# Unread matmuls that hold the TensorE clock: one per tile, spread evenly, in place of a larger demand with a larger carry

## The chip, the cores and the metric

One NeuronCore of one Trainium2 chip. The time is device microseconds from the first to the last instruction. All runs below are fast (run to run spread up to about 1%). A ratio is the one for runs of both kernels from the same rounds on the same chip; it is not quite the ratio of the medians that stand beside it.

Words used throughout: *cold* is a granted TensorE clock of 0.50 in the trace's clock records, *warm* is 1.00; each change in them lies on a multiple of 3.41 us from the first. A *window* is one such stretch of 3.41 us. A *tile* is one pass of the main loop, mostly three PSUM banks of scores and one exponential over 128x1536. An *unread matmul* is a 128x128 by 512 matmul whose result nobody reads; it is there only to keep the clock up. A *tail* is the chain that normalises a head group (three small TensorE steps with VectorE between, some two tiles apart).

## The reference, cut to what matters

```python
x = A_x                                            # 2048 x 640, bf16; 32 heads of 20
x = x + _A_ref(_layernorm(x), A_wqkv, A_wo)        # layer 0: window of 256 keys
x = x + _B_ref(_layernorm(x), B_wqkv, B_wo)        # layer 1: all 2048 keys, no mask
x = x + _A_ref(_layernorm(x), A_wqkv, A_wo)        # layer 2
x = x + _B_ref(_layernorm(x), B_wqkv, B_wo)        # layer 3
```

## The kernel before

All four layers are woven into one list of tiles. A tile's scores are matmuls of 32 rows (a head of 20, padded), its products with the values matmuls of 21 columns (32\*128 and 128\*21 on the page). A *full-array* matmul, below, is a projection, an output product or an unread matmul: 128\*128 on the page, with 320 or 512 moving columns. Everything else, projections, layernorms and tails, is a list of generators that `pump` advances a little in every tile. The bookkeeping counts full-array work as `heat`, and `keep_clock` adds unread matmuls where it falls short:

```python
def advance(task):
    ...
    state["heat"] += n / 0.22 * (0.15 if task in tails else 0.7 if task.name[0] == "ln" else 1.0)

def keep_clock(least):
    while state["heat"] < least:
        t = choose(False)                       # real work first
        if t is not None and state["credit"] > -0.5:
            state["credit"] -= advance(t)
            continue
        b = min(mfree, key=mfree.get)           # a spare PSUM bank: two early on, then one
        if mfree[b][0] > state["tick"]:
            return                              # taken, by a tail for instance: no unread matmul
        nc.tensor.matmul(ps[:, b, :], lhsT=ident[:], rhs=masks[:, 0, :], start=True, stop=True)
        state["heat"] += 1.0

# in the loop over tiles, after the scores and the exponential of a tile of n_b banks:
    r = rate(t)
    pump(r, r + 0.1)
    ...
    state["heat"] += 0.414 * n_b                # scores and values are counted too
    if woven <= state["unit"] < index[3, 1, 0, None]:   # from layer 1's first tiles to the last layer
        keep_clock(1.0 * n_b - surplus)
    surplus = min(max(surplus + state["heat"] - 1.0 * n_b, 0.0), 1.0 * n_b)
    state["heat"] = 0.0
```

So a tile of three banks asks for 3 - 3 x 0.414 = 1.76 full-array matmuls, and a surplus of up to 3 is carried over.

The softmax here doesn't subtract the row's maximum and nothing guards it: scores larger than these inputs give would overflow.

## Time and profile before

| | before |
|---|---|
| time, median of 3 | 2382.0 us (2379.2 to 2386.25) |
| ScalarE busy | 2183.4 us, 92% of the profiled span of 2378.9 us |
| TensorE busy | 1980.5 us, 83% |
| mean granted clock | 0.82 |
| unread matmuls in the program | 549 |

ScalarE's exponentials are the bound. What is to be won or lost is ScalarE's idle time. The prediction shows the page's lines and the busy times by stage.

### The profile page before, as it was taken

How to read it: one execution, taken by the hardware profiler on the slowest of the kernel's cores; microseconds unless marked ns; L12 is line 12 of the kernel's file. 1: busy time of each engine (PE TensorE's matmuls, PEld its weight loads, DVE VectorE, ACT ScalarE, POOL GpSimd, SP SyncE). 2: the span in 40 equal slices, each digit the busy share in tenths (PEclk: the TensorE clock that was granted, in tenths of full speed). 3: DMA queues.
4: the chain of work that ended last, by engine and by line, in shares of the span. 5: the costliest groups of instructions: out<-in, count | busy, mean ns of one | idle time of the engine just before them, and what ended most of it. 6: DMA issues, size and time to landing. Idle time of an engine off the chain costs nothing. (4 is left out here: it accounts for less than half of the span.)

```text
span 2378.9 us, 39796 instructions
## 1 busy us (share of the span) xinstructions
PE 1980.5 (83%) x15407; PEld 707.1 (30%) x15554; DVE 1458.8 (61%) x2724; ACT 2183.4 (92%) x1739; POOL 142.5 (6%) x295
## 2 busy tenths in 40 slices
PE   7888988878888888778888888887788788888887
PEld 3443333323322332223322333232221121112122
DVE  7576776425646666656666554452567777777774
ACT  7787889898999999999899999999999989999997
POOL 3110110000000001000110001001000000000000
PEclk9898999997988999999997999899755565556557
DMA  6232422322200223102330034112200010001100
GB/s 183 72 101 63 113 67 59 76 70 64 82 19 26 57 67 93 37 14 54 82 98 20 15 82 113 31 33 75 64 29 26 26 37 26 26 27 37 38 14 12
DMA packets 173678, 132.53 MB, mean 56 GB/s; under 512 B 115760, under 2 KB 156080, under 8 KB 173488
## 3 DMA queue, kind: packets, MB, share of 16 engines
q1 hardware_dynamic: 163872, 101.39, 16.9%
q0 software_dynamic: 9616, 28.59, 3.5%
q8 instruction: 122, 2.00, 0.3%
q14 instruction: 68, 0.56, 0.1%
HBM read 98.70 MB, written 27.79 MB: 53 GB/s over the span
## 5 line engine op out<-in xcount | busy, mean ns | idle before, releaser
L1252 ACT ACTIVATE pt<-ps 128x1536 bf16<-128x1536 f32 (+3 forms) x1584 | 2033.7, 1425 | 149.2 <-PE ps L1221 136.9
L1221 PE MATMUL ps<-qt,kt 32*128 32x512 bf16 x4008 | 657.8, 470 | 214.1 <-ACT pt L1252 153.6
L1288 PE MATMUL ps<-pt,vt 128*21 128x512 bf16 x3688 | 473.1, 464 | 22.9 <-DVE oT L810 13.9
L1221 PEld LDWEIGHTS <-kt 32*128 32x128 bf16 x4008 | 188.9, 94 | 622.2 <-issue 601.3
L1318 DVE TENSOR_TENSOR pt<-pt,masks 128x1024 bf16<-128x1024 bf16 (+5 forms) x403 | 238.9, 625 | 133.4 <-ACT pt L1252 132.8
L353 PE MATMUL ps<-xnT,wqk 128*128 128x512 bf16 x760 | 215.6, 395 | 31.1 <-DMA wqk<-in_B_wqkv_dram 8.7
L1288 PEld LDWEIGHTS <-vt 128*21 128x21 bf16 x3960 | 104.0, 90 | 372.3 <-issue 364.1
L304 DVE CAST st<-ps 128x512 bf16<-128x512 f32 x127 | 87.7, 690 | 165.2 <-PE ps L353 164.2
L530 PE MATMUL ps<-wop,on 128*128 128x320 bf16 x976 | 173.1, 322 | 8.0 <-DVE rz L995 2.8
L613 PE MATMUL ps<-masks,ident 128*128 128x512 bf16 x473 | 167.7, 417 | 6.8 <-issue 3.3
L1221 PE MATMUL ps<-qa,ka 32*128 32x384 bf16 (+2 forms) x1408 | 119.1, 280 | 38.0 <-ACT pt L1252 32.7
L1252 ACT ACTIVATE ka<-ps 128x2048 bf16<-128x2048 f32 x68 | 133.6, 1965 | 2.6 <-PE ps L1221 2.2
L858 DVE TENSOR_SCALAR xnT<-ps 128x512 int32<-128x512 f32 x88 | 60.8, 691 | 120.9 <-PE ps L851 119.6
L1020 DVE TENSOR_TENSOR on<-oT,ps 128x512 bf16<-128x512 bf16 x128 | 87.3, 682 | 64.0 <-PE ps L1016 60.8
L539 DVE TENSOR_TENSOR x_sb<-x_sb,ps 128x320 bf16<-128x320 bf16 x120 | 57.8, 482 | 110.0 <-PE ps L530 109.6
L444 PE MATMUL ps<-wv,xnT 128*128 128x320 bf16 x640 | 113.1, 311 | 7.5 <-DVE va L304 1.5
L810 DVE CAST oT<-ps 128x512 bf16<-128x512 f32 x112 | 76.8, 686 | 67.5 <-PE ps L1288 48.1
L530 PEld LDWEIGHTS <-on 128*128 128x128 bf16 x976 | 91.8, 103 | 77.0 <-issue 40.9
L353 PEld LDWEIGHTS <-wqk 128*128 128x128 bf16 x830 | 72.6, 99 | 124.4 <-issue 54.0
L1288 PE MATMUL ps<-pt,va 128*21 128x384 bf16 (+2 forms) x1408 | 78.9, 287 | 10.7 <-DVE oT L810 4.9
L1221 PEld LDWEIGHTS <-ka 32*128 32x128 bf16 x1408 | 44.8, 92 | 106.5 <-issue 97.8
L1288 PE MATMUL ps<-ka,vt 128*21 128x512 bf16 x272 | 70.0, 600 | 2.6 <-DVE oT L810 1.9
(105 smaller groups left out, 1623.7 us busy)
## 6 DMA issues: line engine op xcount, KB each, us to landing
vt<-v_d SPq DMA_DIRECT2D x48, 336.0 KB
kt<-k_d SPq DMA_DIRECT2D x192, 80.0 KB
wqk<-in_B_wqkv_dram SPq DMA_DIRECT2D x80, 160.0 KB
wqk<-in_A_wqkv_dram SPq DMA_DIRECT2D x70, 160.0 KB
k_d<-st POOLq DMA_DIRECT2D x75, 128.0 KB, 2.2
q_d<-st POOLq DMA_DIRECT2D x75, 128.0 KB, 2.1
qt<-q_d SPq DMA_DIRECT2D x384, 20.0 KB
v_d<-vs POOLq DMA_DIRECT2D x16, 336.0 KB, 3.5
```

What stands on the lines that cost most here:

```text
L304: nc.vector.tensor_copy(out=out_, in_=in_)
L353: nc.tensor.matmul(pq, lhsT=wt[:, dc, :], rhs=xt[:, dc, :], start=(dc == 0), stop=(dc == KD - 1),)
L444: nc.tensor.matmul(pv, lhsT=xt[:, dc, i * P : (i + 1) * P], rhs=wv_sb[l % 2][:, dc, h * HD : (h + 1) * HD], start=(dc == 0), stop=(dc == K ...
L530: nc.tensor.matmul(yp, lhsT=on[:, g, qb * P : (qb + 1) * P], rhs=wop[:, g, i * HD : (i + 1) * HD], start=(g == g0), stop=(g == G - 1),)
L613: nc.tensor.matmul(ps[:, b, :], lhsT=ident[:], rhs=masks[:, 0, :], start=True, stop=True)
L810: nc.vector.tensor_copy(out=oT[:], in_=op)
L858: V.tensor_scalar(out=xi.bitcast(I32)[:, i * C : (i + 1) * C], in0=side["psum"], scalar1=SCALE * LOG2E * E23, scalar2=127.0 * E23, op0=ALU ...
L1020: nc.vector.tensor_tensor(out=on[:, g, :], in0=oT[:], in1=zb, op=ALU.mult)
L1221: nc.tensor.matmul(sp[:, i, col * P : (col + qn) * P], lhsT=u.k(kc, j), rhs=u.q(j, q0, qn), start=True, stop=True,)
L1252: nc.scalar.activation(out=pt[:, i:k, b0 * P :], in_=sp[:, i:k, b0 * P :], func=ACT.Exp, scale=SCALE,)
L1288: nc.tensor.matmul(op[32 * j : 32 * j + VW, q0 * P : (q0 + qn) * P], lhsT=u.v(kc, j), rhs=pg[:, i, col * P : (col + qn) * P], start=(first ...
L1318: nc.vector.tensor_tensor(out=pt_[:, i:k, b0 * P :], in0=pt_[:, i:k, b0 * P :], in1=mv_, op=ALU.mult,)
```

## The change

The intent: no tile without a full-array matmul. Scores and values no longer count; every tile of three banks asks for one, in the first layers as well; at most one is carried over; and where a tail holds the spare bank, the unread matmul is written into the tail's own bank just ahead of the tail's result.

```diff
+    def cool():
+        return state["heat"] + state["carry"] < state["least"]
   ... (unread(b): the matmul of before, and heat + 1)
+    def warm_bank(b):
+        if cool() and (
+            state["credit"] <= 0.0 or all(task.wake > state["tick"] for task in todo)
+        ):
+            unread(b)
-    def keep_clock(least):
-        while state["heat"] < least:
+    def keep_clock():
+        while cool():
   ...
+        spare = state["heat"] + state["carry"] - state["least"]
+        state["carry"] = min(max(spare, 0.0), 1.0)
+        state["heat"] = 0.0
   ... (t_tail, at each of its three steps)
         mb = yield from take_m()
+        warm_bank(mb)
   ... (the loop)
+                state["least"] = n_b / 3 if state["unit"] < index[3, 1, 0, None] else 0.0
                 load_ahead()
   ...
-                state["heat"] += 0.414 * n_b
-                if woven <= state["unit"] < index[3, 1, 0, None]:
-                    keep_clock(1.0 * n_b - surplus)
-                surplus = min(max(surplus + state["heat"] - 1.0 * n_b, 0.0), 1.0 * n_b)
-                state["heat"] = 0.0
+                keep_clock()
```

More of the change, by code (lines that the diff above doesn't have):

```diff
@@ L176 @@
     tails = []
-    state = {"tick": 0, "held": None, "credit": 0.0, "early": True, "act": True, "unit": 0, "heat": 0.0}
+    state = {"tick": 0, "held": None, "credit": 0.0, "early": True, "act": True, "unit": 0, "heat": 0.0, "carry": 0.0, "least": 0.0}
     class Task:
@@ L601, in push_layer, with unread @@
                 push(("v", l, c), t_v(l, c, (0, 1)), need[0], 5.6)
-    def keep_clock(least):
-        while state["heat"] < least:
+    def cool():
+        return state["heat"] + state["carry"] < state["least"]
+    def unread(b):
+        nc.tensor.matmul(
+            ps[:, b, :], lhsT=ident[:], rhs=masks[:, 0, :], start=True, stop=True
+        )
+        state["heat"] += 1.0
+    def warm_bank(b):
[5 more added lines that the diff above has]
+        while cool():
             t = choose(False)
@@ L611, in keep_clock @@
             if mfree[b][0] > state["tick"]:
-                return
-            nc.tensor.matmul(
-                ps[:, b, :], lhsT=ident[:], rhs=masks[:, 0, :], start=True, stop=True
-            )
-            state["heat"] += 1.0
+                break
+            unread(b)
+        spare = state["heat"] + state["carry"] - state["least"]
+        state["carry"] = min(max(spare, 0.0), 1.0)
+        state["heat"] = 0.0
     def key_blocks(l, part):
@@ L1004, in t_tail @@
         mb = yield from take_m()
+        warm_bank(mb)
         rp = ps[0:32, mb, :].bitcast(BF16)[:, 0:P]
@@ L1013, in t_tail @@
         mb = yield from take_m()
+        warm_bank(mb)
         zb = ps[:, mb, :]
@@ L1179 @@
         wide_pt = 0
-        surplus = 0.0
         started = set()
```

## The prediction

> **What bounds the kernel now.** I read the page first, its busy times and its 40 slices:
>
> ```profile
> PE 1980.5 (83%) x15407; PEld 707.1 (30%) x15554; DVE 1458.8 (61%) x2724; ACT 2183.4 (92%) x1739; POOL 142.5 (6%) x295
> ...
> ACT  7787889898999999999899999999999989999997
> ...
> PEclk9898999997988999999997999899755565556557
> ```
>
> ScalarE is busy 92% of the span: the exponentials bound the kernel, and time can be won only where ScalarE is idle, 196 us in all (2378.9 less 2183.4). The third line is the clock that the throttle granted to TensorE. It is near full for 28 slices and about half in the last 12, where the kernel asks for no unread matmuls. Next I read busy times by stage (columns: stretch, length, busy us of PE, PEld, DVE, ACT, POOL, clock, DMA share, GB/s):
>
> ```profile
> 0.00:240.00 240.00, 205.22 (x1773) 91.66 (x1793) 162.18 (x402) 179.60 (x223) 46.66 (x110) 0.91 0.38 105
> 240.00:480.00 240.00, 214.04 (x1880) 86.32 (x1907) 147.75 (x311) 212.45 (x184) 28.03 (x54) 0.99 0.30 79
> 480.00:720.00 240.00, 202.07 (x1528) 71.07 (x1549) 119.74 (x243) 227.50 (x186) 10.79 (x20) 0.87 0.22 58
> 720.00:960.00 240.00, 198.36 (x1639) 76.47 (x1657) 153.12 (x290) 226.42 (x179) 16.04 (x32) 0.95 0.24 62
> 960.00:1200.00 240.00, 197.67 (x1644) 75.83 (x1660) 146.48 (x275) 225.36 (x170) 10.64 (x22) 0.94 0.19 48
> 1200.00:1440.00 240.00, 203.63 (x1700) 75.77 (x1720) 141.47 (x277) 225.98 (x170) 14.53 (x29) 0.90 0.23 56
> 1440.00:1690.00 250.00, 202.95 (x1722) 76.38 (x1742) 102.40 (x214) 238.16 (x176) 15.85 (x29) 0.92 0.22 60
> 1690.00:2379.00 689.00, 556.55 (x3545) 153.66 (x3543) 485.62 (x717) 647.91 (x458) 0.00 (x0) 0.56 0.09 29
> ```
>
> ScalarE's idle time is the length less its busy time: 60.4 us in the first stage, 94.1 us from 240 to 1690 us, 41.1 us in the last. The last stage has ScalarE at 94% with the clock at 0.56, so a low clock costs nearly nothing where TensorE has only scores and values to multiply. The change does not touch that stage.
>
> The trace has the clock's records: it is 1.00 or 0.50 and switches at multiples of 3.41 us. Before 240 us there are 5 cold intervals (41 us, ScalarE idle 20.4 us of them). Starting in 240 to 1690 us there are 30 (212 us, ScalarE idle 34.1 us); the warm 1238 us of that stage have 60.0 us idle, 4.8%. At that rate 212 us would have 10.3 us idle anyway, so **cold costs at most about 24 us there**. That is the pot, an estimate from idle time.
>
> What sets the clock? I counted, in each 3.41 us window of the trace, the matmuls that use all 128 rows and columns (512 moving columns = 1). After a warm window with none, the clock fell 26 times in 29; with one, 9 in 26; with two, 7 in 55; with 2.5 to 3, once in 45; with four or more, never. After a cold window the clock rose 5 times in 19 with one, 5 in 19 with two, 5 in 10 with three, 27 in 31 with four or more. Of the seven windows with two that fell, four had only 4 to 6 value matmuls besides, where 8 are usual, so the packed matmuls seem to count a little. One example shows how a hole arises (all engines, then the unread matmuls' line alone; in the second fence the columns are PE, PEld, clock, DMA share, GB/s):
>
> ```profile
> 1017.10:1058.10 41.00, 32.14 (x304) 11.83 (x305) 24.29 (x44) 41.00 (x32) 0.00 (x0) 1.00 0.07 20
> 1256.00:1259.50 3.50, 2.44 (x30) 1.04 (x27) 3.36 (x9) 3.50 (x5) 0.00 (x0) 0.99 0.00 0
> 1259.50:1269.70 10.20, 9.63 (x50) 2.20 (x50) 6.95 (x10) 9.36 (x8) 0.00 (x0) 0.50 0.01 2
> ```
>
> ```profile
> 1017.10:1058.10 41.00, 11.38 (x36) 2.55 (x41) 1.00 0.07 20
> 1256.00:1259.50 3.50, 0.00 (x0) 0.00 (x0) 0.99 0.00 0
> 1259.50:1269.70 10.20, 3.70 (x7) 0.52 (x8) 0.50 0.01 2
> ```
>
> The timeline there shows tails (the normalising steps after a head group) holding the one spare bank: two unread matmuls at 1255.3 us, then none until 1261.6 us. The window from 1256 us has TensorE busy 70% with packed work, and the next is cold for 10.2 us, in which ScalarE loses 0.8 us. From 1017 to 1058 us, 36 unread matmuls were issued and ScalarE was never idle: unread matmuls cost nothing where they stand.
>
> [...] the last stage has TensorE 81% busy (556.6 of 689 us) at 0.56: busy with packed matmuls is not enough. [...]
>
> **The change part by part.** I compared the two programs' instruction orders; the sequence of exponentials is identical, so every tile can be placed at the time it has in the old trace.
>
> - *Demand.* Before, 0.586 of a matmul per bank was missing (1.76 in a three-bank tile), with a surplus of up to 3 carried. Now it is 1 per three-bank tile and 1 carried. The built unread matmuls fall from 549 to 448, so 101 fewer. The old trace's group of them is busy 167.7 us for 473 records, 0.355 us each, so that is 36 us less TensorE work; but it stood where ScalarE is 95 to 100% busy, so I book 0 us.
> - *First layers.* Before 240 us the count goes from 5 to 8. The projections already give more than one matmul per tile, and the bookkeeping counts transposes as activity, so the cold intervals at 54, 99 and 143 us have the same order as before around them; at 184 us one projection matmul moves in, at 222 us one or two unread ones go. I book 0 us of the 20.4 us.
> - *Distribution.* Between 480 and 1690 us, stretches between two exponentials with no full-array matmul fall from 229 to 114. In 240 to 1690 us, gaps without one above 3.4 us fall from 52 to 22; most of those left lie at transposes. Around the 30 cold starts, about 22 to 24 have their hole filled ("2, tail, none, none, tail" becomes "1, 1, 1, 1, 1"), and 6 to 8 (337, 583, 727, 863, 1071, 1150, 1372 us) do not.
> - *Risk inside.* A tile takes some 1.4 to 1.6 us, so one per tile is two, sometimes three, per window. About 100 windows would sit at two; at 7 falls in 55, less since most have 8 or more value matmuls beside them (I take half), that is about 6 new falls. Rewarming is slower with two than with three or four per window.
> - *Tails' banks.* One unread matmul (0.355 us as above) ahead of a tail's matmuls; a tail's steps are two tiles apart, so 0 us.
>
> Sum: 30 cold starts become about 30 - 23 + 6 = 13. The pot of 24 us, by starts, gives 24 x 17/30 = 13.6 us saved. I take off 4 us for slower rewarming (about 13 starts, a third of them one window of 3.4 us longer with some 15% extra idle is 2 us, doubled as I trust it little): **net about -10 us, 2372 us.**
>
> **Rivals.**
> (a) *Too thin.* Two per window is the edge: one recorded fall in eight. If sustained stretches fall at that rate, new falls are 12 or more and rewarming is slow, cold time stays at 212 us or grows, and the time is 2380 to 2395 us. For it: the table of falls at two. Against it: four of those seven windows had few value matmuls beside them, and a fifth had its matmuls at the window's edge.
> (b) *All of the pot.* Holes filled, stretches stay warm: cold only at transposes, -20 us, 2362 us.
> (c) *TensorE relieved.* 101 fewer matmuls in front of scores, worth up to 36 us if scores were late because of them; against it, ScalarE's idle 0.0 of 41 us where they are densest.
> (d) *Something else becomes the bound anyway.* A saved ScalarE wait is given back at the next projection-heavy stretch, where ScalarE waits for TensorE at full clock (60 us of idle in warm intervals). Then 2380 us.
>
> **Range and chances.** The whole pot is about 1% of the time and the three runs of before spread by 0.3% (2379.2 to 2386.25), so neither side of 2% is near: faster by over 2% needs 48 us, twice the pot, and slower by over 2% would need cold to spread to stages that are bound by TensorE. I take 2372 us, 2357 to 2388, with 0.03 faster, 0.96 same, 0.01 slower.
>
> **What would show it.** In the changed profile: 448 unread matmuls built (fewer in the records), spread singly; clock from 480 to 1690 us near 0.95 in place of 0.87 to 0.95; cold starts in 240 to 1690 us about 13, mostly at transposes; ScalarE's idle there from 94 to about 84 us; the first 240 us and the last 690 us alike. The prediction is wrong if cold starts stay near 30 (rival a), if the first stage's clock rises clearly above 0.91, or if the clock rises and ScalarE's idle does not fall (rival d).

## The result, and the profile after

2461.79 us median of 4 runs (2443.42 to 2464.2) against 2380.7 (2379.2 to 2386.25); ratio 1.0308, 95% interval 1.0267 to 1.035. Slower by 3.1%, where 2372 us had been forecast: outside the range, and on the wrong side.

The page of the changed kernel, the same three lines as the prediction shows of the kernel before (busy times; tenths of ScalarE's busy time in 40 slices; tenths of the granted clock):

```profile
PE 2103.4 (86%) x15310; PEld 712.1 (29%) x15453; DVE 1462.8 (60%) x2724; ACT 2202.4 (90%) x1739; POOL 142.5 (6%) x295
...
ACT  6777989898988998889899889989999989999997
...
PEclk9899997967955899658998589859665565556557
```

The clock drops to five and six tenths again and again in the middle, where it had stood at eight and nine. TensorE is busy for 123 us more (2103.4 less 1980.5), although 101 matmuls fewer are in the program. Busy times by stage (stretch, length, busy us of PE, PEld, DVE, ACT, POOL, clock, DMA share, GB/s):

```profile
0.00:240.00 240.00, 205.54 (x1795) 92.74 (x1815) 164.83 (x407) 182.36 (x225) 47.78 (x112) 0.93 0.39 107
240.00:480.00 240.00, 214.53 (x1805) 83.66 (x1828) 143.57 (x303) 206.77 (x178) 25.28 (x48) 0.91 0.29 74
480.00:720.00 240.00, 210.99 (x1395) 67.17 (x1413) 114.14 (x231) 213.75 (x170) 12.40 (x23) 0.72 0.23 59
720.00:960.00 240.00, 211.83 (x1503) 72.67 (x1513) 137.13 (x258) 215.20 (x171) 12.27 (x25) 0.78 0.21 52
960.00:1200.00 240.00, 210.20 (x1524) 67.87 (x1541) 138.21 (x263) 217.02 (x162) 5.62 (x11) 0.72 0.15 39
1200.00:1440.00 240.00, 206.07 (x1597) 71.46 (x1618) 147.41 (x278) 215.69 (x160) 16.04 (x32) 0.81 0.22 53
1440.00:1690.00 250.00, 223.33 (x1709) 80.33 (x1727) 109.46 (x222) 228.61 (x165) 18.81 (x36) 0.82 0.25 62
```

From 480 to 1440 us the clock is 0.72 to 0.81 (before: 0.87 to 0.95), and ScalarE has 8 to 14 us less work in each 240 us. The clock records of 240 to 1690 us say how: **16 cold starts in place of 30, but 601 cold us in place of 212**. The starts became fewer (forecast: 13). The cold intervals became long: 150, 120, 82, 75 and 68 us are the longest; in the kernel before none of that stage was over 21 us.

**Where the 79 us went.** The two programs have the same 1652 exponentials in the same order, so the start of the n-th can be compared. The first 160 take 274.2 us before and 271.6 after; the next 1040 take 1423.3 and 1504.0 us; the rest 668.1 and 669.1 us. All of the loss, 81 us, is in the middle. There ScalarE is idle for 150.3 us in place of 88.7 (62 us); the other 19 us are in its busy time (1353.7 less 1334.6), since an exponential that has to wait for its scores does not begin under the end of the one before: in the traces one alone is busy for 1.45 us, three in a row for 3.79 us.

The longest cold interval, exponentials 445 to 553, in both kernels (same columns as above; the kernel before first):

```profile
651.70:778.50 126.80, 106.82 (x833) 34.99 (x843) 71.50 (x142) 121.12 (x109) 0.00 (x0) 0.87 0.07 22
```

```profile
666.40:816.60 150.20, 139.76 (x808) 34.81 (x820) 72.90 (x142) 126.73 (x108) 0.00 (x0) 0.50 0.07 18
```

The same work takes 23.4 us longer. TensorE is busy 93% of the stretch after, at half the clock: it has become the bound, and ScalarE waits. The waits of that stretch in the changed kernel name it (who waited, for whom, us in total, times, longest):

```profile
ACT pt L1272 <- PE ps L1241: 20.5, 56, 1.5
```

20.5 us in 56 waits of the exponentials for their scores. The same row of the same stretch in the kernel before:

```profile
ACT pt L1252 <- PE ps L1221: 4.1, 10, 0.6
```

**A flaw in how I had counted.** The prediction's table of falls and rises came from the records of matmuls. These are not complete. The groups of the unread matmuls, the kernel before and then the changed one (busy us, mean ns, idle before and its releasers):

```profile
L613 PE MATMUL ps<-masks,ident 128*128 128x512 bf16 x473 | 167.7, 417 | 6.8 <-issue 3.3 <-DVE on L1020 1.3 <-DVE rT L1008 0.7
L613 PEld LDWEIGHTS <-ident 128*128 128x128 bf16 x549 | 36.2, 98 | 78.9 <-issue 77.5
```

```profile
L609 PE MATMUL ps<-masks,ident 128*128 128x512 bf16 x371 | 201.1, 542 | 13.6 <-DVE on L1041 9.8 <-DVE rT L1028 2.4 <-DVE rz L1014 0.3
L609 PEld LDWEIGHTS <-ident 128*128 128x128 bf16 x448 | 45.0, 100 | 163.4 <-issue 163.0
```

In these programs every matmul has its own weight load (976 and 976 records at L530, for one), and the weight loads number 549 and 448, just as many as the programs hold; the matmul records lack 76 and 77 (so the 36 unread matmuls of the prediction's example from 1017 us on are 41). Counted by weight loads, the share of 3.41 us windows after which the clock changed is (a projection or unread matmul counts 1, a 320-column one 0.625, rounded):

| full-array matmuls in the window | 0 | 1 | 2 | 3 | 4 | 5 | 6 and more |
|---|---|---|---|---|---|---|---|
| warm, fell next: before | 25 of 29 | 3 of 12 | 14 of 64 | 0 of 33 | 0 of 58 | 1 of 87 | 0 of 160 |
| warm, fell next: after | 14 of 17 | 7 of 16 | 6 of 39 | 1 of 34 | 1 of 29 | 0 of 66 | 0 of 145 |
| cold, rose next: before | 1 of 170 | 0 of 3 | 13 of 39 | 1 of 4 | 5 of 7 | 16 of 20 | 6 of 6 |
| cold, rose next: after | 1 of 167 | 0 of 28 | **0 of 107** | 4 of 33 | 5 of 11 | 15 of 20 | 3 of 3 |

What held a warm clock in these traces (with two it fell after 6 windows of 39 in the changed kernel) did not bring back a cold one (with two it rose after none of 107). One matmul per tile is about two per window.

### The profile page after: what moved, and what is told of

It is laid out like the page before. It is cut to its first block, busy times and chain, and to the rows that moved or that the text cites. A ratio compares the mean times of both kernels' runs of the same rounds, so it can differ in the third digit from the quotient of the medians.

```text
span 2457.9 us, 39598 instructions
## 1 busy us (share of the span) xinstructions
PE 2103.4 (86%) x15310; PEld 712.1 (29%) x15453; DVE 1462.8 (60%) x2724; ACT 2202.4 (90%) x1739; POOL 142.5 (6%) x295
## 5 line engine op out<-in xcount | busy, mean ns | idle before, releaser
L1241 PE MATMUL ps<-qt,kt 32*128 32x512 bf16 x4008 | 700.8, 500 | 176.9 <-ACT pt L1272 123.7
L1304 PE MATMUL ps<-pt,vt 128*21 128x512 bf16 x3688 | 502.2, 493 | 24.8 <-DVE oT L828 15.0
L1241 PEld LDWEIGHTS <-kt 32*128 32x128 bf16 x4008 | 179.7, 96 | 609.8 <-issue 595.8
L609 PE MATMUL ps<-masks,ident 128*128 128x512 bf16 x371 | 201.1, 542 | 13.6 <-DVE on L1041 9.8
L530 PE MATMUL ps<-wop,on 128*128 128x320 bf16 x976 | 175.1, 325 | 7.9 <-DVE on L1041 3.1
L1241 PE MATMUL ps<-qa,ka 32*128 32x384 bf16 (+2 forms) x1408 | 135.4, 319 | 23.4 <-ACT pt L1272 21.3
L530 PEld LDWEIGHTS <-on 128*128 128x128 bf16 x976 | 92.6, 104 | 78.4 <-issue 42.0
L1304 PE MATMUL ps<-pt,va 128*21 128x384 bf16 (+2 forms) x1408 | 92.3, 329 | 9.4 <-DVE oT L828 4.3
L609 PEld LDWEIGHTS <-ident 128*128 128x128 bf16 x448 | 45.0, 100 | 163.4 <-issue 163.0
L1037 PE MATMUL ps<-rT,spread 32*128 32x128 bf16 x512 | 64.8, 264 | 14.8 <-issue 9.5
```

The lines of the kernel that those rows point to most:

```text
L530: nc.tensor.matmul(yp, lhsT=on[:, g, qb * P : (qb + 1) * P], rhs=wop[:, g, i * HD : (i + 1) * HD], start=(g == g0), stop=(g == G - 1),)
L1037: nc.tensor.matmul(zb[:, qb * P : (qb + 1) * P], lhsT=spread4[:, qb, :], rhs=rT[:], start=True, stop=True,)
L1241: nc.tensor.matmul(sp[:, i, col * P : (col + qn) * P], lhsT=u.k(kc, j), rhs=u.q(j, q0, qn), start=True, stop=True,)
L1304: nc.tensor.matmul(op[32 * j : 32 * j + VW, q0 * P : (q0 + qn) * P], lhsT=u.v(kc, j), rhs=pg[:, i, col * P : (col + qn) * P], start=(first ...
```

## The experiments

**Theories.** First: *no recovery*. At two per window, spread singly, a cold clock did not come up (none of 107 in the table), so each fall lasts until projections come by; the lowered demand is the cause. Rival one: *the tails' banks*, where an unread matmul stands ahead of the tail's own work. Rival two: *the spread or the small carry*. Rival three, which came up on the way: *unread matmuls under a cold clock*, not the cold clock, are what costs.

The counts of unread matmuls in most of the expectations include nine fills at the very end that all versions have; without them the programs hold 253 (level_alone), 838 (level_kept), 307 (no_tail_banks), 751 (bursts), 396 (pairs), 640 (level_kept_no_tail_banks), 860 (level_kept_transposes), 448 (tail_short), 665 (level_1p35), 1121 (level_2p4) and 713 (level_kept_carry3). All runs gave the right result. "Middle" is exponentials 160 to 1200, as above; cold us and ScalarE's idle us are those of the middle in the profiled run.

| run | median us | ratio to before (95%) | middle | cold | ScalarE idle |
|---|---|---|---|---|---|
| before | 2381 | 1 | 1423.3 | 220 | 88.7 |
| changed | 2461.8 | 1.031 (1.027 to 1.035) | 1504.0 | 635 | 150.3 |
| level_alone | 2444.4 | 1.025 (1.022 to 1.028) | 1485.2 | 747 | 137.5 |
| level_kept | 2361.5 | 0.990 (0.986 to 0.994) | 1410.6 | 82 | 77.8 |
| no_tail_banks | 2412.2 | 1.012 (1.009 to 1.014) | 1456.1 | 651 | 110.6 |
| bursts | 2427.8 | 1.016 (1.011 to 1.021) | 1470.4 | 247 | 128.9 |
| no_unread | 2413.8 | 1.013 (1.010 to 1.017) | 1461.7 | 778 | 124.7 |
| pairs | 2419.1 | 1.015 (1.012 to 1.019) | 1466.0 | 528 | 123.4 |
| level_kept_no_tail_banks | 2381.4 | 1.000 (0.997 to 1.004) | 1422.0 | 223 | 86.3 |
| level_kept_transposes | 2361.9 | 0.992 (0.989 to 0.995) | 1404.3 | 58 | 72.1 |
| tail_short | 2439.9 | 1.023 (1.020 to 1.026) | 1480.8 | 666 | 130.5 |
| level_1p35 | 2382.5 | 0.998 (0.995 to 1.002) | 1429.8 | 151 | 94.9 |
| level_2p4 | 2366.7 | 0.992 (0.989 to 0.995) | 1408.4 | 37 | 73.7 |
| level_kept_carry3 | 2361.7 | 0.989 (0.986 to 0.993) | 1406.9 | 71 | 77.2 |
| tails_only | 2451.6 | 1.030 (1.026 to 1.033) | 1482.6 | 753 | 138.8 |

The changed kernel was timed in rounds of its own, the experiments in four others (medians of before 2384.7, 2383.0, 2386.0 and 2385.0 us). Where the text below compares medians of the changed kernel with theirs, a difference of 100, 50, 48 or 22 us is 97, 45, 41 or 20 us by the ratios, and the changed kernel's ratio alone is good to 0.4%, 10 us. The last three columns are of one profiled run each, which lies up to 12 us from the median of its kernel.

**1. The demand lowered alone** (level_alone), in the kernel before:

```diff
-                state["heat"] += 0.414 * n_b
                 if woven <= state["unit"] < index[3, 1, 0, None]:
-                    keep_clock(1.0 * n_b - surplus)
-                surplus = min(max(surplus + state["heat"] - 1.0 * n_b, 0.0), 1.0 * n_b)
+                    keep_clock(n_b / 3 - surplus)
+                surplus = min(max(surplus + state["heat"] - n_b / 3, 0.0), 1.0 * n_b)
```

> The kernel before with one thing changed: the demand, a third of a matmul per bank in place of 0.586 (surplus of up to three, no tails' banks, no unread ones in the first layers, all as before); 262 unread matmuls built in place of 549. Theory (a cold clock does not recover at about two full-array matmuls per 3.41 us window, so the lowered demand lengthens cold stretches): cold time between 240 us and the end of the demand at least the 601 us of the changed kernel, time 2455 to 2490 us. Rival (the demand is harmless, and the tails' banks or the small carry cost the time): 2375 to 2390 us.

2444 us, 11 us under the band of the theory and 54 us above its rival's. Cold as expected. The lowered demand alone makes the kernel slow, without any of the change's other parts.

**2. The demand kept** (level_kept), in the changed kernel:

```diff
-                state["least"] = n_b / 3 if state["unit"] < index[3, 1, 0, None] else 0.0
+                state["least"] = 0.586 * n_b if state["unit"] < index[3, 1, 0, None] else 0.0
```

> The changed kernel with the demand of before (0.586 per bank, 1.76 per three-bank tile), carry of one, tails' banks and first layers as changed; 847 unread matmuls built. Theory: clock recovers within a few windows, holes are filled as well, so time 2360 to 2378 us, at or under before. Rival (tails' banks or carry cost the time): stays at 2440 us or more. Second rival (too many matmuls on TensorE): 2390 to 2420 us with a full clock.

2361 us, as the theory had it: 1.0% under before and 100 us under the changed kernel, by one constant. The stages in the profile, 480 to 960 us:

```profile
480.00:720.00 240.00, 212.81 (x1639) 75.91 (x1640) 122.47 (x246) 231.09 (x190) 10.48 (x22) 0.97 0.23 61
720.00:960.00 240.00, 213.85 (x1699) 80.03 (x1698) 152.05 (x290) 226.01 (x178) 15.54 (x31) 0.96 0.24 61
```

The clock is 0.97 and 0.96; TensorE is as busy as in the changed kernel (211 and 212 us), but with nearly twice as many unread matmuls done in the program, and ScalarE gets its scores (idle 77.8 us in the middle, against 150.3).

**3. Without the tails' banks** (no_tail_banks): the three calls of `warm_bank` taken out of the changed kernel.

> The changed kernel without unread matmuls in the tails' banks, demand of one per tile kept; 316 built in place of 448. Theory: more holes and still no recovery, so 2460 to 2490 us. Rival (an unread matmul ahead of a tail's own work delays the tail and what follows): time falls by 20 us or more.

2412 us: here the theory failed and the rival was right. As cold as the changed kernel (651 and 635 us), and yet 50 us faster. A cold clock is not the whole cause.

**4. Bursts** (bursts): the changed kernel, five more asked for in every sixteenth tile.

```diff
+                if t % 16 == 0:
+                    state["burst"] = 5.0
-                state["least"] = n_b / 3 if ...
+                state["least"] = n_b / 3 + state["burst"] if ...   # burst is dropped once it is met
```

The four per window that the expectation asks for are my estimate from the prediction's counts (a cold clock rose after 27 of 31 windows with four or more, 5 of 10 with three, 5 of 19 with two); a threshold was not shown.

> The changed kernel, demand of one per tile kept, and every sixteenth tile (some 23 us) asks for five more in one tile; 760 built. Theory: recovery needs four or more in one window and a burst gives it, so no cold stretch lasts beyond about 25 us, cold time between 240 us and the end of the demand falls from 601 to 150 to 250 us, time 2375 to 2400 us. Rival (the evenly spread single matmuls themselves cost the time, by standing ahead of scores): 2440 us or more.

The clock did as expected (247 us cold), the time did not: 2428 us. The burst costs by itself. Between two 128x1536 exponentials with no full-array work but unread matmuls, the start-to-start time under a warm clock is 1.33 us in the median with none, one or two unread matmuls near, and 2.24 us with six; under a cold one it is 3.29 us with six. The cases with six are few, about ten cold ones and fewer warm ones, so the warm figure is rough.

**5. No unread matmul at all** (no_unread): `state["least"] = 0.0` in the changed kernel.

> The changed kernel with no unread matmul asked for at all (demand zero everywhere). In the long cold stretches of the runs so far, a tile of one 1536-column exponential with no unread matmul near it took 1.35 to 1.38 us (median and mean, demand lowered alone), against 1.33 us warm, and 1.5 to 1.65 us with one. Theory now (a cold clock alone costs little; unread matmuls issued under a cold clock are what costs, because TensorE then becomes the bound): cold time between 240 and the last layer rises to 900 us or more, and yet the time is 2385 to 2415 us, well under the changed kernel. Rival (the cold clock itself is the cost): the idle per cold us of the changed kernel goes on, 2480 us or more.

2414 us, at the upper end of the theory's band (what the expectation calls the theory now is rival three of the list): cold for 778 us of the middle, the longest of all, and 48 us faster than the changed kernel. So the middle is 38 us longer than before by the cold clock without any unread matmul (1461.7 less 1423.3; the kernel before was itself cold for 220 us of it), and 42 us of the changed kernel's loss (1504.0 less 1461.7) come with the unread matmuls. The split is not clean: this run was cold for longer than the changed kernel (778 us against 635), and without a demand `keep_clock` pulls no real work forward, so its projections, transposes and output products stand elsewhere in TensorE's order. Counted by weight loads 400 to 4200 of the scores, a different number of them had gone before at 1085 of 3800 scores than in the changed kernel (in no_tail_banks and tails_only at 3). Exponentials 445 to 553 of this run, a stretch with hardly any such work:

```profile
662.70:786.10 123.40, 102.94 (x730) 30.16 (x726) 71.08 (x141) 120.71 (x110) 0.00 (x0) 0.50 0.08 22
```

Wholly cold, without a single unread matmul, this stretch is faster than in the kernel before (126.8 us) and 26.8 us faster than in the changed one: TensorE is busy 83%, not 93%. The same stretch takes 121.5 us in level_kept (clock 1.00, 149 unread matmuls by weight loads), 134.3 us in no_tail_banks (0.54, 63 of them) and 150.2 us in the changed kernel (0.50, 89). Under a cold clock it is longer with unread matmuls than without; under a warm one 149 of them cost nothing that shows.

**6. Pairs** (pairs): the same demand on average, two in every second tile.

```diff
-                state["least"] = n_b / 3 if ...
+                state["least"] = (2 * n_b / 3 if t % 2 else 0.0) if ...
```

> The changed kernel with the same demand on average, but asked as two in every second tile and none in the others; 405 built (nine of them the fills at the very end) in place of 457. Theory (what counts is how many fall in a window of 3.41 us): nearly the same, 2430 to 2465 us. Rival (two back to back bring the clock up where two apart do not, as the cold windows with two suggest: 13 of 39 rose in the kernel before, none of 107 in the changed one): cold time from 601 to under 350 us and 2395 to 2420 us.

2419 us, at the upper end of the rival's band, but with 528 us cold (495 between 240 and 1690 us), well above its 350: half right. After cold windows with two full-array matmuls the clock rose 15 times in 65, against 0 in 107 with the singles. Some of these windows hold projections too. Of the cold windows whose only full-array work was two unread matmuls, the clock rose after 14 of 48 where the two stood together (weight loads under 0.7 us apart) and after none of 14 where they stood apart, in this one run; in the kernel before it rose after 11 of 33, all together, and in the changed kernel after none of 104, all apart. So grouping does help the recovery; why, the runs do not show.

**7. The demand kept, without the tails' banks** (level_kept_no_tail_banks): edits 2 and 3 together.

> The changed kernel with the demand of before (1.76 per three-bank tile) and without the tails' banks: 649 built. Theory: under a warm clock an unread matmul in a tail's bank costs nothing and fills holes, so without them there are more falls, 2363 to 2380 us, no faster than with them (2361 us). Rival (an unread matmul ahead of a tail's own work costs time by its place, whatever the clock): 2345 us or less, as 50 us went with them at the low demand.

2381 us, just above the theory's band and far from the rival's. At this demand the tails' banks are worth 20 us, where at the low demand they cost 50: they fill the holes (223 us cold without them, 82 with them; 22 cold starts between 240 and 1690 us and 10), and no cost of theirs shows there.

**8. The transposes not counted** (level_kept_transposes): edit 2, and

```diff
-        ... (0.15 if task in tails else 0.7 if task.name[0] == "ln" else 1.0)
+        ... (0.15 if task in tails else 0.0 if task.name[0] == "ln" else 1.0)
             mb = yield from take_m()
+            warm_bank(mb)
             trp = ps[:, mb, :].bitcast(BF16)...      # the layernorm's transposes
```

By weight loads, in the traces of before and changed, the clock fell after 12 of 19 warm windows with transposes (L408) and no full-array matmul, and after 27 of 27 with neither. In the kernel before, the windows just ahead of the cold intervals at 54.5, 337.9, 863.5 and 1150.2 us held 9 or 10 transposes and no full-array matmul.

> The run with the demand kept, and two more edits: the layernorm's transposes count for nothing in the bookkeeping, and an unread matmul may stand in the bank of each. 869 built. Theory (most falls that are left lie at transposes[...]): fewer falls between 0 and 1690 us than the 16 of the run with the demand kept, 2340 to 2360 us. Rival (ScalarE waits there for the layernorm and its banks, not for the clock, or TensorE is too full): 2360 us or more.

2362 us, no faster than without it. There are fewer falls (12 against 16 up to 1690 us), as the theory said, but in the first 240 us, where cold time fell from 31 us (demand kept) to 24, ScalarE's idle stays at 59 to 61 us. So the wait there did not shrink with the cold time that went; this fits the rival, but 24 cold us are left, and what the wait is for was not traced.

**9. Short ones in the tails' banks** (tail_short): the changed kernel, `warm_bank` with 128 columns in place of 512.

> The changed kernel, the same places and the same bookkeeping, but the unread matmuls in the tails' banks are of 128 columns in place of 512. If it is the array's work under a cold clock that costs (tail work plus an unread matmul in one tile make TensorE the bound), the cost shrinks with the work and the time falls to 2405 to 2435 us, with the cold time unchanged or longer. If it is the place (a matmul ahead of the tail, with its wait and its order, whatever its length), it stays at 2445 us or more.

2440 us, between the bands: 22 of the 50 us that the tails' ones cost go with three quarters of their columns. The rest stays: a short one still has its weight load (0.10 us in the trace) and its 0.27 us as recorded.

**10. Halfway** (level_1p35): demand of `0.45 * n_b`.

> The changed kernel with the demand halfway, 1.35 per three-bank tile (about three per window of 3.41 us); 674 built with the nine fills. After a cold window with three the clock rose in about a quarter of the cases, so cold stretches should end after some four windows: cold time between 240 and 1690 us of 200 to 350 us and 2385 to 2420 us. If the threshold lies below three: near the run with the demand kept, 2360 to 2375 us.

After cold windows with three the clock rose in 1 of 4 (before) and 4 of 33 (changed) in the table above, and in 29% over all fifteen traces; a threshold was not shown.

2382.5 us, under the first band and above the second: cold for less time than expected (151 us), and level with the kernel before. Just 0.35 more per tile than the changed kernel takes 79 us off.

**11. More** (level_2p4): demand of `0.8 * n_b`.

> The changed kernel with more demand than before, 2.4 per three-bank tile; 1130 built. Cold time between 240 and 1690 us at or under the 86 us of the run with the demand kept. If warm unread matmuls stay free: 2355 to 2370 us. If TensorE becomes the bound (about 290 more of 0.2 to 0.36 us, in tiles where ScalarE was the bound): 2375 to 2420 us.

2367 us, in the band for free ones. The clock is better still (37 us cold), the time is not.

**12. The demand kept, carry of three** (level_kept_carry3).

> The run with the demand kept, with a carry of up to three in place of one; 722 built in place of 847. A carry lets two tiles go without after a full one, so some more windows with none: cold time of 100 to 180 us in place of 86 and 2362 to 2378 us. If the small carry is itself a loss (more matmuls for nothing): under 2355 us.

2362 us, at the edge of the first band, but with no more cold time than with a carry of one (71 and 82 us): the carry makes no difference here. This run, level_kept and level_kept_transposes (2361 to 2362 us) are the fastest versions tried, alike within their spread.

**13. The tails' ones alone** (tails_only): `keep_clock` of the changed kernel issues none.

> The changed kernel with unread matmuls in the tails' banks only (177 besides the nine fills), none elsewhere. Without any the time was 2414 us, with all but the tails' 2412 us, with all 2462 us. If the tails' ones cost by their own place (ahead of a tail's matmuls under a cold clock), they cost the same alone: 2450 to 2475 us. If the 50 us come from the sum (every tile has one, no tile is left with room to catch up), they cost much less alone: 2410 to 2435 us.

2452 us, at the lower end of the band for the place. Without any 2414, with all but these 2412: the 177 of this run cost 38 us alone (21 us in the middle of the two profiled runs, which lie 12 us under and 3 us over their medians). In the changed kernel, which holds 141 unread matmuls more than no_tail_banks, they cost 50. So most of the cost is theirs by their own place, and does not need the others.

**Why just those.** I took each pair of 128x1536 exponentials that follow each other under a cold clock, without projections, output products or transposes between, from 480 to 1640 us, and split them by whether a tail step stood in the tile. Mean start-to-start time:

| cold tiles | no tail step | with a tail step |
|---|---|---|
| no_unread | 1.33 us | 1.38 us |
| tails_only | 1.34 us | **1.59 us** |
| no_tail_banks | **1.45 us** | 1.39 us |
| tail_short | **1.48 us** | **1.48 us** |
| changed | **1.51 us** | **1.72 us** |

In the runs with unread matmuls in one kind of tile only, the cost stands in that kind, and it is larger beside a tail step; the short ones of tail_short bring it down there from 1.72 to 1.48 us. ScalarE alone takes 1.33 us per tile (the median start-to-start time without unread matmuls, warm and cold). What a tile of TensorE takes beyond that is lost, and ScalarE, which is the bound in the other tiles, has no room to catch up. Three tiles in the order of TensorE's instructions show it (start, us, engine and line, what, count, idle before and its releaser). First the run without unread matmuls:

```profile
696.00 0.61 PE L1241 MATMUL ps<-qt,kt 32*128 32x512 bf16 x3
696.54 0.26 PE L1009 MATMUL ps<-sel,oT 128*128 128x4 bf16 x4
696.73 0.40 PE L1304 MATMUL ps<-pt,va 128*21 128x256 bf16 x4
697.06 0.61 PE L1241 MATMUL ps<-qt,kt 32*128 32x512 bf16 x3
698.17 0.61 PE L1304 MATMUL ps<-pt,vt 128*21 128x512 bf16 x4 [0.49 <-DVE oT L828]
698.71 0.61 PE L1241 MATMUL ps<-qt,kt 32*128 32x512 bf16 x3
699.25 0.29 PE L1026 MATMUL ps<-ident,hl 128*32 128x128 bf16 x1
699.26 0.71 PE L1304 MATMUL ps<-pt,vt 128*21 128x512 bf16 x4
699.90 0.61 PE L1241 MATMUL ps<-qt,kt 32*128 32x512 bf16 x3
```

The same three tiles of the changed kernel:

```profile
707.00 0.61 PE L1241 MATMUL ps<-qt,kt 32*128 32x512 bf16 x3
707.54 0.61 PE L609 MATMUL ps<-masks,ident 128*128 128x512 bf16 x1
707.94 0.29 PE L1009 MATMUL ps<-sel,oT 128*128 128x4 bf16 x4
708.16 0.40 PE L1304 MATMUL ps<-pt,va 128*21 128x256 bf16 x4
708.49 0.61 PE L1241 MATMUL ps<-qt,kt 32*128 32x512 bf16 x3
709.60 0.61 PE L1304 MATMUL ps<-pt,vt 128*21 128x512 bf16 x4 [0.50 <-DVE oT L828]
710.15 0.61 PE L1241 MATMUL ps<-qt,kt 32*128 32x512 bf16 x3
710.69 0.61 PE L609 MATMUL ps<-masks,ident 128*128 128x512 bf16 x1
711.23 0.29 PE L1026 MATMUL ps<-ident,hl 128*32 128x128 bf16 x1
711.23 0.71 PE L1304 MATMUL ps<-pt,vt 128*21 128x512 bf16 x4
711.88 0.61 PE L1241 MATMUL ps<-qt,kt 32*128 32x512 bf16 x3
```

From the first scores to the fourth it is 3.90 us without and 4.88 us with the two unread matmuls (L609) ahead of tail steps (L1009, L1026): 0.49 us each, and each pushes the values and the next scores (L1241) back by that. Three exponentials need 3 x 1.33 = 3.99 us, so without them TensorE keeps up and with them it doesn't. Under a warm clock there is room: the same tile time is 1.33 us with none, one or two.

## Why the prediction was wrong

Step by step, in the prediction's own order:

- *What bounds the kernel* held: ScalarE, and its idle time as the place to look. One reading beside it was loose: the last stage, called one of only scores and values, also has 208 output products (L530).
- *The pot of 24 us* fits as what cold cost in the kernel before: level_kept, level_2p4 and level_kept_transposes took away 138 to 183 of its 220 cold us, and their middles are 13 to 19 us shorter (level_kept is 23 us under the before of its rounds, by medians of 2361.5 and 2384.7 us). But I took it as an upper bound for a change in either direction, and allowed for more than 6 us worse only in the rival. It bounds what can be gained. Nothing bounded the loss, and "slower by over 2% would need cold to spread to stages that are bound by TensorE" overlooked that a cold clock with unread matmuls made a stage bound by TensorE (exponentials 445 to 553: TensorE busy 93% at 0.50, and 20.5 us of waits for scores).
- *Cold starts* were forecast at 13 and were 16, but this near hit is largely luck: a clock that is cold already cannot fall. There was one start per 41 us of warm time before (30 in 1238) and one per 53 us after (16 in 849); at the old rate 849 warm us would have had 21. That filling holes prevents falls is shown at the larger demand instead (22 starts without the tails' banks, 10 with them). The sign that the prediction gave for rival (a), starts staying near 30, did not come, although its cold clock did.
- ***Rewarming* is the step that failed.** "A third of them one window of 3.4 us longer" was 2 us, doubled to 4. In fact the mean cold interval went from 212/30 = 7 us to 601/16 = 38 us, since after a cold window with two the clock rose in none of 107 cases. In cold time the term stood for some 15 us (a third of 13 starts, 3.4 us each); by the same reckoning it came to 601 less 16 x 7, about 490 us, some thirty times as much. I had a number for it (5 of 19 with two), but from incomplete records, and from a kernel that issued its two back to back; the pairs run shows that this matters (15 of 65).
- *101 fewer matmuls, 0 us, since they cost nothing where they stand* held for warm tiles (level_2p4, with 1121 of them, is 15 us faster than the kernel before in the middle). It was carried over unsaid to cold ones. There an unread matmul of the changed kernel costs up to half a microsecond (0.49 us in the three tiles shown).
- *Tails' banks, 0 us* was wrong for the kernel as changed (50 us, with the demand at one) and too low the other way for the kernel with the demand kept (they gain 20 us).
- *First layers, 0 us* held: the first 160 exponentials take 271.6 us against 274.2.
- *Rivals*: (a), too thin, was the right direction and named slow rewarming; its 2380 to 2395 us was too small by 67 us and more, since it let cold time stay at 212 us or grow without saying how far, and had no cost for unread matmuls under a cold clock. (b), (c) and (d) did not happen.

What is shown: that the demand is the cause (one constant, 100 us; it also sets how much real work `keep_clock` pulls forward, but the stretch of exponentials 445 to 553, with hardly any such work, takes 121.5 us with the one value and 150.2 us with the other); that the recovery fails at it; that a cold clock loses time without any unread matmul and that unread matmuls under a cold clock lose more, mostly in the tails' banks. The sizes, 38 and 42 us of the middle, are a split by two profiled runs whose order of real work also differs. What is left open: why two back to back raise the clock where two apart do not, and why 28 of the tails' 50 us stay with a quarter of the columns; the weight load and the order are candidates, and I did not separate them.

I had taken the clock to rise and to fall at one and the same amount of work, which no trace had shown. In these traces the two are far apart: with two full-array matmuls a warm window was mostly followed by a warm one (fell after 6 of 39 in the changed kernel), a cold one always by a cold one (rose after 0 of 107).

## What to carry to other kernels

A dose of filler matmuls has to be judged by what it does after a fall, not only by how well it prevents one: here two per window mostly held a warm clock (it fell after 6 of 39 in the changed kernel) but, spread singly, raised a cold one after none of 107 windows; with four or five in a window it rose more often than not (54% and 78% over all runs). Filler at one per tile was the worst of three choices here: the middle stayed cold for 635 us, and a cold tile took 1.51 to 1.72 us in place of 1.33 to 1.38; none at all was 48 us faster, and 1.76 per tile 100 us faster. And count instructions by records that are complete, here the weight loads.

## What the traces of all versions show

- Over all fifteen profiled kernels here, by my count of weight loads, a warm clock fell after 79% of windows with no full-array matmul (276 of 351), 51% with one (98 of 191), 21% with two (106 of 499) and 5% with three (28 of 577); a cold one rose after 10% of windows with two (56 of 564), 29% with three, 54% with four, 78% with five and all 80 with six or more. A load at a window's edge moves single cases between neighbours: the cold window from 98.9 us of the kernel before and that from 99.4 us of the changed one hold six loads by their start times, and the clock did not rise after them.
- In no_unread 123.4 us, nearly all packed matmuls of 32 rows or 21 columns, stayed at 0.50 with TensorE busy 83% and no gap above 1.3 us in its records.
- Grouping bears on the recovery: two matmuls asked for in one tile raised a cold clock in 15 of 65 windows with two (pairs), spread singles in none of 107 (changed kernel).
- Filler matmuls cost where they did not lift the clock: a cold tile took 1.33 us without them or a tail step (no_unread), and 1.51 us, or 1.72 with a tail step, in the changed kernel.
- Matmul records were missing where weight-load records were complete: 371 of 448 and 448 of 448 in the changed kernel's trace.
